# Attention scores on quadrants of TensorE's array in a fused attention and MLP kernel

## The chip, the cores and the metric

The kernel runs on one core of one Trainium2 chip. The metric is device time in microseconds of one execution; the time of the kernel before is the median of three runs, 1028.31 us (1028.2 to 1028.95). Engines are named as the profile names them: PE is TensorE's matmul, PEld its weight load, DVE VectorE, ACT ScalarE, POOL GpSimd, SP SyncE, which issues nearly all transfers.

## The reference

Sliding-window attention with a linear bias, and an MLP behind it, all in fp32:

```
batch, heads, seq, head_dim = 8, 8, 576, 64;  window = 128
scores = q @ k.T / 8 + bias        # bias = -slope[head] * (query - key)
scores = -1e9 where not (0 <= query - key < window)
attn   = softmax(scores);  y = attn @ v
x = y as 4608 tokens of 512        # 8 heads of 64 side by side
h = x @ w_in                       # 512 -> 2048
g = h * erf(softplus(h))
out = g @ w_out                    # 2048 -> 512
```

A block of 64 queries needs the keys of its own block of 64 and of the two before it, 192 keys.

## The kernel before, in words

**Units.** The 4608 tokens are 12 chunks of 384. Of every two batches, the first 384 tokens of each make a chunk, and the two remainders of 192 make a third. A chunk has four units, one for each pair of heads; unit u is chunk u // 4 and pair u % 4, 48 in all. A unit has three blocks t of 128 queries, which are two halves of 64. The first block of an ordinary chunk has 128 keys to look at, every other one 192.

**A unit's work** (class `Attention`, method `unit`): the scores of both heads in TensorE (tile `s`, line 459); VectorE adds the bias and takes the row's extreme (L466); ScalarE makes the exponential and its sum (L476); VectorE inverts the sums (L489, L490); GpSimd scales (L499); TensorE transposes (tile `t`, L517), VectorE or ScalarE copies that out (tile `pT`); TensorE multiplies with v (tile `px`, L550); the result is split in a high and a low part as a chunk's x (L560).

**The scores before.** For head j, one product has 128 rows and 128 columns of weights: rows 0 to 63 hold the 64 dimensions of q for the first half of the queries and zeros for the second, rows 64 to 127 the other way round. The moving operand is k twice, the second copy shifted by 64 keys, so that both halves meet their own 192 keys in one product. Two products (two heads) make a block; both write one bank, columns 0 and 256. The host lays out q with its zeros and k twice for each head, 1536 columns a unit (1920 in a third chunk), loaded as one tile `qk`.

**The MLP.** Products with the first six columns of blocks of w_in run beside the attention (tile `h`, L757, and `o`, L820: the first pass); the other ten run in a second pass with fewer, recombined products (L959, L1030). Each fp32 weight is split in high and low parts, mostly on VectorE, for the first pass at the start (L592 to L615). x is also saved to DRAM (tile `xd`) for the second pass.

**What sets the order.** Class `Plan` simulates the engines with a cost for each operation and a due time `at`, and writes the program out in the order that this gives. Each engine then runs its instructions in that order and waits on semaphores. `unit_time(u)` gives a unit's due time; loads are due `LL` = 22 us ahead. The line with `op({"PE": ...}, products, ...)` gives the planner the cost of a block's products; the named buffers of a tag (`Buf`) are taken in the order of use, or, with `keep=0`, by whoever comes first when one is free.

**Banks of PSUM.** Eight: two under tag "h", three under "o0" to "o2", and one each under "s" (scores), "t" (transposes) and "xt" (the product with v). In the first six units (`early`) scores also use "h", and transposes "o1". In the second pass all six of "o0" to "o2", "xt", "s" and "t" collect the output.

**Warm-up.** 40 products on zeros (L394) have the lowest priority; the planner puts them where TensorE would be idle in the first microseconds.

Of the kernel before, what the change touches and what calls it, by code (L numbers as in the profile page):

```python
# [8 lines left out]
F32 = mybir.dt.float32  # L9
# [8 lines left out]
B, H, S, D = 8, 8, 576, 64  # L18
NPAIR = H // 2
P = 128  # L20
WIN = 128
DM = H * D
# [3 lines left out]
CH = 384  # L26
NTT = CH // P
# [14 lines left out]
TE, NE = 5.5, 8  # L42
TA = 6.5
LL, LN, LT = 22, 0.3, 0
LEAD = 45
TMF = 1.2
TM = TMF * 4 * TA / NF1
# [279 lines left out]
def fp32_us(n):  # L327
    return 2 * max(n / 1200.0 + 0.003, 0.111)
# [10 lines left out]
def dma(nbytes, n=1, run=1536, eng="SP", out=False):  # L339
    packet = 9 + 0.0367 * run  # L340
    return dict(costs={eng: n * 0.42}, moved=nbytes / run * packet / 16e3 + 0.05 * n * (run > 2048), packet=packet, after=0.9 if out else 1.8 if run > 2048 else 1.3, count=n)
# [17 lines left out]
class Attention:  # L359
# [43 lines left out]
    def load(self, u):  # L403


        c, g = u // 4, u % 4
        nc, op = self.nc, self.plan.op
        at = unit_time(u) - LL
        last = c % 3 == 2
        n, m = (576, 10) if last else (384, 6)  # L410
        i = c // 3 if last else c - c // 3
        src, vsrc = self.qk[last][i, g], self.v[last][i, g]
        qk = Buf(self.kp, [P, 768 + 2 * 576], F32, "qk", NKB, f"qk{u}")
        v = Buf(self.vp, [P, 10, 2, D], F32, "v", NQ, f"v{u}")
        q = lambda t, j: qk[:, (2 * t + j) * P : (2 * t + j + 1) * P]
        k = lambda j, x, w: qk[:, 768 + j * n + x : 768 + j * n + x + w]
        if u:
            parts = [[qk]] * 3
            op(emit=lambda e: nc.sync.dma_start(qk[:, : 768 + 2 * n], src), w=[qk], at=at,
               **dma(P * (768 + 2 * n) * 4, run=(768 + 2 * n) * 4))  # L420
        else:
            both = lambda x, lo, hi: x[:, 768 : 768 + 2 * n].rearrange("p (j n) -> p j n", j=2)[:, :, lo:hi]
            pieces = [Part(qk, i) for i in range(4)]
            for i, (eng, issue, lo, hi) in enumerate((
                    ("SP", nc.sync, 0, 2 * P), ("Act", nc.scalar, 0, P), ("Act", nc.scalar, P, n), ("SP", nc.sync, 2 * P, 6 * P))):
                get = (lambda x, lo=lo, hi=hi: x[:, lo:hi]) if eng == "SP" else (lambda x, lo=lo, hi=hi: both(x, lo, hi))
                run = (hi - lo) * 4
                op(emit=lambda e, issue=issue, get=get: issue.dma_start(get(qk), get(src)), w=[pieces[i]], at=-30 + i,
                   **dma(P * run * (1 if eng == "SP" else 2), run=run, eng=eng))
            parts = [pieces[:2], pieces, pieces]  # L430
        op(emit=lambda e: nc.sync.dma_start(v[:, :m].rearrange("p x j d -> p (x j d)"), vsrc), w=[v], at=at + 2,
           **dma(P * m * 2 * D * 4, run=m * 2 * D * 4))
        return parts, q, k, v

    def unit(self, u):
# [12 lines left out]
        for t in range(3):  # L448
            c0 = 0 if last or t else 1
            n = (3 - c0) * D  # L450
            off = 192 * t if last else max(0, 128 * t - 64)
            pool, tag, bufs = (self.moe.ps_h, "h", 2) if early and (3 * u + t) % 3 else (self.ps, "s", 1)
            ps = Buf(pool, [P, 2, 256], F32, tag, bufs, f"s{u}_{t}")
            pt = Buf(self.pp, [P, 3, 2, D], F32, "p", PB, f"p{u}_{t}")
            p.append(pt)

            def products(e, ps=ps, t=t, off=off, n=n):
                for j in range(2):
                    nc.tensor.matmul(ps[:, j, :n], lhsT=q(t, j), rhs=k(j, off, n),  # L459
                                     start=True, stop=True)  # L460

            op({"PE": 2 * fp32_us(n) + 0.005}, products, r=loaded[t], w=[ps], at=at)

            def biased(e, ps=ps, pt=pt, t=t, c0=c0, n=n):
                for j in range(2):
                    nc.vector.tensor_tensor_reduce(  # L466
                        out=pt[:, c0:, j, :], in0=ps[:, j, :n].rearrange("p (c d) -> p c d", d=D),
                        in1=self.bias[g][:, j, 0::3] if c0 else self.bias[g][:, j, 1:],
                        scale=-0.125, scalar=3.0e38, op0=ALU.add, op1=ALU.min,
                        accum_out=low[t][:, j : j + 1],  # L470
                    )

            def exps(e, pt=pt, t=t, c0=c0):
                for j in range(2):
                    dst = pt[:, c0:, j, :]
                    nc.scalar.activation(dst, dst, AF.Exp, bias=low[t][:, j : j + 1], scale=-1.0,  # L476
                                         accum_out=sums[t][:, j : j + 1])

            op({"DVE": 2 * (0.07 + n * 0.0011)}, biased, r=[ps, self.bias[g]], w=[pt, low[t]], at=at)
            op({"Act": 2 * (0.285 + n * 0.00082)}, exps, tail=0.1, r=[pt, low[t]], w=[pt, sums[t]], at=at)  # L480

        at += LN
# [25 lines left out]
        parts = []  # L508
        for t in range(3):
            c0 = 0 if last or t else 1  # L510
            tag = "o1" if early and t % 2 else "t"
            ps = Buf(self.moe.ps_o if tag == "o1" else self.ps, [P, 512], F32, tag, 1, f"t{u}_{t}")

            def transposes(e, t=t, c0=c0, ps=ps):
                two = ps[:, : 2 * 192].rearrange("p (l c) -> p l c", c=192)
                for cb in range(c0, 3):
                    nc.tensor.matmul(  # L517
                        two[:, :, (2 - cb) * D : (3 - cb) * D],
                        lhsT=p[t][:, cb].rearrange("p j d -> p (j d)"), rhs=self.ident[:, :],
                        is_transpose=True, start=True, stop=True)  # L520

            op({"PE": 0.109 * (3 - c0) + 0.005}, transposes, r=[p[t]], w=[ps], at=at)
            w = (3 - c0) * D
            step, x = (192, t * 384) if not last else ((192, 0), (192, 576), (576, 384))[t]
            part = Part(pT, slice(None), t)
            parts.append(part)

            def out(e, ps=ps, w=w, step=step, x=x):
                two = ps[:, : 2 * 192].rearrange("p (l c) -> p l c", c=192)
                self.copy(e, run(x, 2, step)[:, :, :w], two[:, :, :w])  # L530

            op({"DVE": dve(2 * w), "Act": act(2 * w, src=0.053)}, out, r=[ps], w=[part], at=at)

        px = Buf(self.ps, [P, 512], F32, "xt", 1, f"px{u}")
        if last:
            todo = [[(3 * s, kk, 5 * s + kk) for s in range(2) for kk in (2, 0, 1, 3, 4)]]
        else:
# [154 lines left out]
class Moe:  # L692
# [223 lines left out]
    def second_pass(self, weights, pool2, gone, time):  # L916
# [6 lines left out]
        tiles = []  # L923
        for c in range(nc2):
            x = xs
            po = [Buf(pool, [P, DM], F32, tag, 1, f"p{tag}_{c}") for pool, tag in (
                *((self.ps_o, f"o{t}") for t in range(NTT)), *((self.ps_a, t) for t in ("xt", "s", "t")))]
            for j in range(npair):
                at = time(c * npair + j)
                if j == 1 and c + 1 < nc2:  # L930
# [196 lines left out]
def _layout(q, k, v, moe_w_in, moe_w_out):  # L1127
# [2 lines left out]
    nb = q.shape[0]  # L1130
    nch = nb * S // CH
    qT, kT = (np.ascontiguousarray(a.transpose(0, 1, 3, 2)).reshape(nb, NPAIR, 2, D, S) for a in (q, k))
    qs = np.zeros((nch, NPAIR, 2, D, 3, 2, 2, D), np.float32)
    k_a = np.zeros((nb, NPAIR, 2, D, 2, 2 * WIN + P), np.float32)
    k_c = np.zeros((nb // 2, NPAIR, 2, D, 2, 3, 192), np.float32)
    vs = np.zeros((nb, NPAIR, 2, D, S // D, 2, D), np.float32)
    heads = lambda a: a.transpose(0, 2, 1, 3)
    for b in range(nb):
        m, s = b // 2, b % 2
        for half in range(2):  # L1140
            for t in range(4):
                x = 64 * (2 * t + half)
                to = (3 * m + s, t) if t < 3 else (3 * m + 2, s)
                qs[to[0], :, half, :, to[1], :, half] = heads(qT[b, ..., x : x + 64])
            k_a[b, :, half, :, :, 64 * (1 - half) :] = heads(kT[b, ..., : 320 + 64 * half])
            x = 256 + 64 * half
            k_c[m, :, half, :, :, s] = heads(kT[b, ..., x : x + 192])
        qs[3 * m + 2, :, s, :, 2, :, s] = heads(qT[b, ..., 512:])
        k_c[m, :, s, :, :, 2] = heads(kT[b, ..., 384:])
        for j in range(2):  # L1150
            vs[b, :, j, :, :, j] = v[b, j::2].reshape(NPAIR, S // D, D, D).transpose(0, 2, 1, 3)
    qs = qs.reshape(nb // 2, 3, NPAIR, P, 768)
    qk_a = np.concatenate([qs[:, :2].reshape(nb, NPAIR, P, 768), k_a.reshape(nb, NPAIR, P, 768)], 3)
    qk_c = np.concatenate([qs[:, 2], k_c.reshape(nb // 2, NPAIR, P, 1152)], 3)
    v_a = np.ascontiguousarray(vs[..., :6, :, :]).reshape(nb, NPAIR, P, 768)
    v_c = np.concatenate([vs[s::2, ..., 4:, :, :].reshape(nb // 2, NPAIR, P, 640) for s in range(2)], 3)
    bits = lambda a: a.view(np.int64)
# [29 lines left out]
```

## Time and profile before

| | |
|---|---|
| median of three runs | 1028.31 us |
| profiled execution, its own time | 1027.85 us |
| its span | 1026.1 us |
| TensorE busy (PE) | 1010.0 us, 98% |
| weight loads (PEld) | 925.9 us, 90% |
| VectorE | 646.0 us, 63% |
| ScalarE | 647.3 us, 63% |
| GpSimd | 162.9 us, 16% |
| last score on TensorE | 464.5 us |
| moved by DMA | 191 MB, mean 186 GB/s |
| granted TensorE clock | 1.00 throughout |

The profiled execution's time is 1.75 us over its span, which runs from the first instruction to the last. Rows of the timeline give the start in us, the length in us, engine, line and operation, tile written and tiles read, the shape of the product (rows times columns of weights), the moving operand, and how many instructions were merged. A product in fp32 shows as two weight loads and two matmul rows; one in the rounded form (fp32r, the MLP's) as one of each. The length of a matmul row is modelled and reaches into its successor's; distances between starts say how fast rows follow each other.

### The profile page before, as it was taken

The numbers are of one execution on the slowest core, as the hardware profiler recorded it, in microseconds if no ns is written. First come the engines' busy times: TensorE is split into PE (matmuls) and PEld (weight loads), VectorE is DVE, ScalarE is ACT, GpSimd is POOL, SyncE is SP. The second block draws the span as 40 slices with busy tenths as digits, with TensorE's granted clock in tenths as the row PEclk, the third lists the DMA queues.
The fourth block names the chain that finished last, engine by engine and source line by source line (L and its number), as shares of the span: only waits on it lengthen the run. The fifth ranks groups of instructions, "written<-read, shape, count | busy, mean of one in ns | idle before, by whom it ended". The sixth has DMA issues, their size and how long they took to land.

```text
span 1026.1 us, 16045 instructions
## 1 busy us (share of the span) xinstructions
PE 1010.0 (98%) x5612; PEld 925.9 (90%) x5612; DVE 646.0 (63%) x1554; ACT 647.3 (63%) x1302; POOL 162.9 (16%) x294
## 2 busy tenths in 40 slices
PE   9899999999999999999999999999999999999998
PEld 8889999888999899999999989889989899899896
DVE  4999888778888645546356547447456456454433
ACT  5788668666787657565557664664665655555543
POOL 3454442225342232211000000000000000000000
PEclk9999999999999999999999999999999999999999
DMA  9865879788969554545778333323323324320402
GB/s 369 331 211 196 306 238 320 243 305 289 345 238 346 174 195 159 181 159 190 291 279 307 124 110 116 113 97 130 113 84 143 113 72 148 121 64 29 124 1 72
DMA packets 63761, 190.98 MB, mean 186 GB/s; under 512 B 7105, under 2 KB 7873, under 8 KB 63681
## 3 DMA queue, kind: packets, MB, share of 16 engines
q1 hardware_dynamic: 62992, 189.43, 52.6%
q8 instruction: 45, 0.74, 0.3%
q10 hardware_dynamic: 688, 0.52, 0.2%
q14 instruction: 36, 0.29, 0.1%
HBM read 137.76 MB, written 52.17 MB: 185 GB/s over the span
## 4 chain that ended last, share of the span: by engine, by line
PE 81%; DVE 12%; DMA 3%; issue 2%; ACT 1%; POOL 0%; DVEq 0%; POOLq 0%; SPq 0%; ACTq 0%
PE pa L959 12%; PE po L1030 12%; PE o L820 11%; PE h L757 10%; PE pc L959 6%; PE px L550 5%; PE s L459 5%; PE pxt L1030 4%; PE pt L1030 4%; PE ps L1030 4%; PE pb L959 3%; DVE p L466 3%; PE t L517 2%; PE warm_ps L394 1%; DMA wd<-wto 1%
## 5 line engine op out<-in xcount | busy, mean ns | idle before, releaser
L499 POOL TENSOR_SCALAR p<-p,st 128x192 f32<-128x192 f32 (+1 forms) x288 | 162.2, 581 | 306.4 <-DVE st L490 204.9
L757 PE MATMUL h<-x,wi 128*128 128x384 f32 x864 | 175.7, 345 | 0.3 <-DVE st L466 0.3
L740 ACT COPY hs<-pa 128x384 f32<-128x384 f32 x115 | 55.2, 480 | 175.0 <-PE pa L959 175.0
L757 PEld LDWEIGHTS h<-x,wi 128*128 128x128 f32 x864 | 150.5, 188 | 3.4 <-PE s L459 0.5
L476 ACT ACTIVATE p<-p,st 128x192 f32<-128x192 f32 (+1 forms) x288 | 124.9, 436 | 41.7 <-DVE st L466 41.3
L820 PE MATMUL o<-wo,gh 128*128 128x512 f32 x432 | 145.5, 418 | 0.0
L459 PE MATMUL s<-qk 128*128 128x192 f32 (+1 forms) x576 | 110.5, 316 | 2.5 <-DVE st L466 2.0
L959 PE MATMUL pa<-t,p 128*128 128x384 f32 x540 | 108.4, 335 | 0.0
L550 PEld LDWEIGHTS px<-pT,v 128*128 128x128 f32 x704 | 100.7, 191 | 3.2 <-DVE pT L401 1.2
L550 PE MATMUL px<-pT,v 128*128 128x192 f32 (+2 forms) x704 | 102.6, 295 | 0.6 <-DVE pT L401 0.4
L1010 DVE TENSOR_TENSOR hs<-s,hs 128x768 f32<-128x768 f32 x60 | 54.8, 953 | 72.3 <-ACT s L1002 72.3
L959 PEld LDWEIGHTS pa<-t,p 128*128 128x128 f32 x540 | 95.5, 187 | 3.4 <-ACT hs L740 0.3
L459 PEld LDWEIGHTS s<-qk 128*128 128x128 f32 x576 | 90.9, 190 | 7.5 <-issue 2.7
L1030 PE MATMUL po<-ho,gh 128*128 128x512 f32 x270 | 90.8, 390 | 0.0
L970 DVE TENSOR_TENSOR hs<-pc,hs 128x384 f32<-128x384 f32 x60 | 33.4, 557 | 90.0 <-PE pc L959 48.7
L466 DVE CUSTOM_DVE_ANT_0 p<-s,bias 128x192 f32<-128x192 f32 x224 | 70.4, 351 | 29.0 <-PE s L459 22.7
L820 PE MATMUL o<-wo,gl 128*128 128x512 f32 x216 | 85.3, 395 | 0.0
L820 PEld LDWEIGHTS o<-wo,gh 128*128 128x128 f32 x432 | 75.4, 189 | 7.1
L517 PE MATMUL t<-ident,p 128*128 128x128 f32 x400 | 67.2, 274 | 7.5 <-POOL p L499 4.0
L1030 PE MATMUL po<-ho,gl 128*128 128x512 f32 x180 | 71.4, 397 | 0.0
L399 ACT COPY pT<-t 128x384 f32<-128x384 f32 (+1 forms) x87 | 39.5, 455 | 48.0 <-PE t L517 40.4
L517 PEld LDWEIGHTS t<-ident,p 128*128 128x128 f32 x400 | 50.2, 144 | 18.5 <-POOL p L499 8.0
(272 smaller groups left out, 1825.5 us busy)
## 6 DMA issues: line engine op xcount, KB each, us to landing
qk<-qk_a SPq DMA_DIRECT2D x31, 768.0 KB, 6.7
xd<-x SPq DMA_DIRECT2D x24, 768.0 KB, 6.0
qk<-qk_c SPq DMA_DIRECT2D x16, 960.0 KB, 5.9
v<-v_a SPq DMA_DIRECT2D x32, 384.0 KB, 4.4
v<-v_c SPq DMA_DIRECT2D x16, 640.0 KB, 4.3
pd<-ot SPq DMA_DIRECT2D x36, 256.0 KB, 3.8
out<-pd SPq DMA_DIRECT2D x36, 256.0 KB, 3.4
p<-wd SPq DMA_DIRECT2D x35, 256.0 KB, 5.0
```

The costliest lines, as they stand in the source:

```text
L459: nc.tensor.matmul(ps[:, j, :n], lhsT=q(t, j), rhs=k(j, off, n), start=True, stop=True)
L466: nc.vector.tensor_tensor_reduce(out=pt[:, c0:, j, :], in0=ps[:, j, :n].rearrange("p (c d) -> p c d", d=D), in1=self.bias[g][:, j, 0::3] i ...
L476: nc.scalar.activation(dst, dst, AF.Exp, bias=low[t][:, j : j + 1], scale=-1.0, accum_out=sums[t][:, j : j + 1])
L499: nc.gpsimd.tensor_scalar(dst, dst, sums[t][:, j : j + 1], 1.0, op0=ALU.mult, op1=ALU.mult)
L517: nc.tensor.matmul(two[:, :, (2 - cb) * D : (3 - cb) * D], lhsT=p[t][:, cb].rearrange("p j d -> p (j d)"), rhs=self.ident[:, :], is_transp ...
L550: nc.tensor.matmul(px[:, to : to + m * D], lhsT=v[:, blk].rearrange("p j d -> p (j d)"), rhs=run(src, m, 256)[:, :, :D], start=first and x ...
L740: self.nc.scalar.copy(out, src)
L757: nc.tensor.matmul(ps[:, :CH], lhsT=ww[:, cs], rhs=xx[:, k], start=(k2 + k + n == 0), stop=(k2 + k + n == 4),)
L820: nc.tensor.matmul(po.all, lhsT=g[:, j, cs], rhs=w.all, start=(u["start"] and n == 0), stop=(u["end"] and n == 2),)
L959: nc.tensor.matmul(dst[:, :CH], lhsT=wv[i](k), rhs=xb[l][:, k], start=start and k + n == 0, stop=k + n == 3, skip_group_check=not start)
L1010: op({"DVE": dve(2 * CH)}, lambda e, s=s, hs=hs: V.tensor_tensor(hs.all, s.all, hs.all, ALU.mult), r=[s, *parts], w=parts, at=at, port=True)
L1030: nc.tensor.matmul(po.all, lhsT=g[:, k, cs], rhs=w.all, start=start and n == 0, stop=end and n == 2)
```

## The change

For each block, four products take the place of two, one for each pair of head j and half h. Head j's q and k lie in rows 64 j to 64 j + 63 of the tile `qk`, once and without zeros. The weights are 64 dimensions by 64 queries, the moving operand 64 dimensions by 192 (or 128) keys, and the product lies on the quadrant of the array that its rows (head) and its output's partitions (half) give. The four are written in the order (j, h) = (0, 0), (1, 0), (0, 1), (1, 1). Each head has its own bank, so a block takes two. The planner's cost for a block is now `SQ` (0.2) plus that of one product in place of two.

A unit's load has 832 columns (384 of q, 448 of k, the first 64 of k zeros) in place of 1536, and in a third chunk 1024 in place of 1920. The first unit's load is still cut in four pieces, the first two of which the first block needs.

The three banks "s", "t" and "xt" become one tag "a" of three, taken by whichever operation comes and finds enough free: two for scores, one for a transpose, one for the product with v. In the first six units scores go in turn to "a", to the two of "h", and to "o0" and "o2". VectorE's biasing reads one bank for each head. The shapes of all other operations stay.

```diff
+SQ = 0.2
...
-        n, m = (576, 10) if last else (384, 6)
+        n, m = (640, 10) if last else (448, 6)
...
-        qk = Buf(self.kp, [P, 768 + 2 * 576], F32, "qk", NKB, f"qk{u}")
+        qk = Buf(self.kp, [P, CH + 640], F32, "qk", NKB, f"qk{u}")
...
-        q = lambda t, j: qk[:, (2 * t + j) * P : (2 * t + j + 1) * P]
-        k = lambda j, x, w: qk[:, 768 + j * n + x : 768 + j * n + x + w]
+        rows = lambda j: slice(j * D, (j + 1) * D)
+        q = lambda t, j, h: qk[rows(j), t * P + h * D : t * P + (h + 1) * D]
+        k = lambda j, x, w: qk[rows(j), CH + x : CH + x + w]
...
-            op(emit=lambda e: nc.sync.dma_start(qk[:, : 768 + 2 * n], src), w=[qk], at=at,
-               **dma(P * (768 + 2 * n) * 4, run=(768 + 2 * n) * 4))
+            op(emit=lambda e: nc.sync.dma_start(qk[:, : CH + n], src), w=[qk], at=at, **dma(P * (CH + n) * 4, run=(CH + n) * 4))
...
-            off = 192 * t if last else max(0, 128 * t - 64)
-            pool, tag, bufs = (self.moe.ps_h, "h", 2) if early and (3 * u + t) % 3 else (self.ps, "s", 1)
-            ps = Buf(pool, [P, 2, 256], F32, tag, bufs, f"s{u}_{t}")
+            if last:
+                off = [320 * t, 320 * t + D] if t < 2 else [P, 320 + P]
+            else:
+                off = [max(0, t * P - D) + x for x in (0, D)]
+            place = (0, 1, 2)[(3 * u + t) % 3] if early else 0
+            if place == 0:
+                ps = [Buf(self.ps, [P, 512], F32, "a", 3, f"s{u}_{t}{j}", keep=0) for j in range(2)]
+            elif place == 1:
+                ps = [Buf(self.moe.ps_h, [P, 512], F32, "h", 2, f"s{u}_{t}{j}") for j in range(2)]
+            else:
+                ps = [Buf(self.moe.ps_o, [P, 512], F32, f"o{2 * j}", 1, f"s{u}_{t}{j}") for j in range(2)]
...
-                for j in range(2):
-                    nc.tensor.matmul(ps[:, j, :n], lhsT=q(t, j), rhs=k(j, off, n),
-                                     start=True, stop=True)
-
-            op({"PE": 2 * fp32_us(n) + 0.005}, products, r=loaded[t], w=[ps], at=at)
+                for h in range(2):
+                    for j in range(2):
+                        nc.tensor.matmul(ps[j][h * D : (h + 1) * D, :n], lhsT=q(t, j, h), rhs=k(j, off[h], n),
+                                         start=True, stop=True)
+
+            op({"PE": SQ + fp32_us(n)}, products, r=loaded[t], w=ps, at=at)
...
-                        out=pt[:, c0:, j, :], in0=ps[:, j, :n].rearrange("p (c d) -> p c d", d=D),
+                        out=pt[:, c0:, j, :], in0=ps[j][:, :n].rearrange("p (c d) -> p c d", d=D),
...
-            tag = "o1" if early and t % 2 else "t"
-            ps = Buf(self.moe.ps_o if tag == "o1" else self.ps, [P, 512], F32, tag, 1, f"t{u}_{t}")
+            spare = early and t % 2
+            ps = Buf(self.moe.ps_o, [P, 512], F32, "o1", 1, f"t{u}_{t}") if spare else Buf(
+                self.ps, [P, 512], F32, "a", 3, f"t{u}_{t}", keep=0)
...
-        px = Buf(self.ps, [P, 512], F32, "xt", 1, f"px{u}")
+        px = Buf(self.ps, [P, 512], F32, "a", 3, f"px{u}", keep=0)
...
+    gap = np.zeros((nb, NPAIR, 2, D, D), np.float32)
+    qk_a = flat(np.concatenate([qT[..., :CH], gap, kT[..., :CH]], 4))
```

More of the change, by code (lines that the diff above doesn't have):

```diff
@@ L409, in load @@
         last = c % 3 == 2
-        n, m = (576, 10) if last else (384, 6)
+        n, m = (640, 10) if last else (448, 6)
         i = c // 3 if last else c - c // 3
         src, vsrc = self.qk[last][i, g], self.v[last][i, g]
-        qk = Buf(self.kp, [P, 768 + 2 * 576], F32, "qk", NKB, f"qk{u}")
+        qk = Buf(self.kp, [P, CH + 640], F32, "qk", NKB, f"qk{u}")
         v = Buf(self.vp, [P, 10, 2, D], F32, "v", NQ, f"v{u}")
-        q = lambda t, j: qk[:, (2 * t + j) * P : (2 * t + j + 1) * P]
-        k = lambda j, x, w: qk[:, 768 + j * n + x : 768 + j * n + x + w]
+        rows = lambda j: slice(j * D, (j + 1) * D)
+        q = lambda t, j, h: qk[rows(j), t * P + h * D : t * P + (h + 1) * D]
+        k = lambda j, x, w: qk[rows(j), CH + x : CH + x + w]
         if u:
             parts = [[qk]] * 3
-            op(emit=lambda e: nc.sync.dma_start(qk[:, : 768 + 2 * n], src), w=[qk], at=at,
-               **dma(P * (768 + 2 * n) * 4, run=(768 + 2 * n) * 4))
+            op(emit=lambda e: nc.sync.dma_start(qk[:, : CH + n], src), w=[qk], at=at, **dma(P * (CH + n) * 4, run=(CH + n) * 4))
         else:
-            both = lambda x, lo, hi: x[:, 768 : 768 + 2 * n].rearrange("p (j n) -> p j n", j=2)[:, :, lo:hi]
             pieces = [Part(qk, i) for i in range(4)]
             for i, (eng, issue, lo, hi) in enumerate((
[L425 to L429, printed above, removed]
+                    ("SP", nc.sync, 0, P), ("Act", nc.scalar, CH, CH + 192), ("Act", nc.scalar, CH + 192, CH + n), ("SP", nc.sync, P, CH))):
+                op(emit=lambda e, issue=issue, lo=lo, hi=hi: issue.dma_start(qk[:, lo:hi], src[:, lo:hi]), w=[pieces[i]], at=-30 + i,
+                   **dma(P * (hi - lo) * 4, run=(hi - lo) * 4, eng=eng))
             parts = [pieces[:2], pieces, pieces]
@@ L477, in exps @@
                                          accum_out=sums[t][:, j : j + 1])
-            op({"DVE": 2 * (0.07 + n * 0.0011)}, biased, r=[ps, self.bias[g]], w=[pt, low[t]], at=at)
+            op({"DVE": 2 * (0.07 + n * 0.0011)}, biased, r=[*ps, self.bias[g]], w=[pt, low[t]], at=at)
             op({"Act": 2 * (0.285 + n * 0.00082)}, exps, tail=0.1, r=[pt, low[t]], w=[pt, sums[t]], at=at)
@@ L925, in second_pass @@
             x = xs
-            po = [Buf(pool, [P, DM], F32, tag, 1, f"p{tag}_{c}") for pool, tag in (
-                *((self.ps_o, f"o{t}") for t in range(NTT)), *((self.ps_a, t) for t in ("xt", "s", "t")))]
+            po = [Buf(self.ps_o, [P, DM], F32, f"o{t}", 1, f"po{t}_{c}") for t in range(NTT)]
+            po += [Buf(self.ps_a, [P, DM], F32, "a", 3, f"pa{t}_{c}", keep=0) for t in range(NTT)]
             for j in range(npair):
@@ L1132, in _layout @@
     qT, kT = (np.ascontiguousarray(a.transpose(0, 1, 3, 2)).reshape(nb, NPAIR, 2, D, S) for a in (q, k))
-    qs = np.zeros((nch, NPAIR, 2, D, 3, 2, 2, D), np.float32)
-    k_a = np.zeros((nb, NPAIR, 2, D, 2, 2 * WIN + P), np.float32)
-    k_c = np.zeros((nb // 2, NPAIR, 2, D, 2, 3, 192), np.float32)
+    flat = lambda a: a.reshape(a.shape[0], NPAIR, P, a.shape[-1])
+    gap = np.zeros((nb, NPAIR, 2, D, D), np.float32)
+    qk_a = flat(np.concatenate([qT[..., :CH], gap, kT[..., :CH]], 4))
+    both = lambda a, lo, hi: [a[s::2, ..., lo:hi] for s in range(2)]
+    qk_c = flat(np.concatenate([*both(qT, CH, 512), *both(qT, 512, S), *both(kT, 256, S)], 4))
     vs = np.zeros((nb, NPAIR, 2, D, S // D, 2, D), np.float32)
-    heads = lambda a: a.transpose(0, 2, 1, 3)
     for b in range(nb):
[L1139 to L1149, printed above, removed]
         for j in range(2):
             vs[b, :, j, :, :, j] = v[b, j::2].reshape(NPAIR, S // D, D, D).transpose(0, 2, 1, 3)
-    qs = qs.reshape(nb // 2, 3, NPAIR, P, 768)
-    qk_a = np.concatenate([qs[:, :2].reshape(nb, NPAIR, P, 768), k_a.reshape(nb, NPAIR, P, 768)], 3)
-    qk_c = np.concatenate([qs[:, 2], k_c.reshape(nb // 2, NPAIR, P, 1152)], 3)
     v_a = np.ascontiguousarray(vs[..., :6, :, :]).reshape(nb, NPAIR, P, 768)
```

## The prediction

> **What bounds the kernel now.** I read the windows by stage first, then the page's chain, then the timeline of TensorE around single score blocks, and last the waits.
>
> ```profile
> core 0: us, PE busy (x) PEld busy (x) DVE busy (x) ACT busy (x) POOL busy (x), PEclk, DMA share, GB/s
> 0.00:25.00 25.00, 23.04 (x161) 22.35 (x162) 11.88 (x65) 14.93 (x52) 8.16 (x24) 1.00 0.94 368
> 25.00:100.00 75.00, 70.03 (x440) 65.16 (x439) 74.41 (x237) 59.26 (x165) 32.05 (x45) 1.00 0.66 241
> 100.00:475.00 375.00, 369.94 (x2258) 344.69 (x2257) 270.97 (x863) 260.68 (x681) 122.66 (x226) 1.00 0.72 252
> 475.00:1026.10 551.10, 547.00 (x2760) 493.70 (x2758) 288.79 (x392) 312.48 (x405) 0.00 (x0) 1.00 0.37 125
> ```
>
> Each row is a stretch; after the times come busy us and instructions per engine. Up to 25 us TensorE is filled up with warm-up products and the DMA engines are 0.94 busy. From 25 to 100 us VectorE has 74.41 of 75 us: it sets the pace, TensorE has 5 us free. From 100 us on TensorE is 98.7% busy, so there a microsecond of its work is a microsecond of the end. Behind 475 us no score is left. The scores alone, in the same stretches:
>
> ```profile
> 0.00:25.00 25.00, 6.07 (x36) 5.33 (x36) 1.00 0.94 368
> 25.00:100.00 75.00, 21.27 (x111) 17.24 (x112) 1.00 0.66 241
> 100.00:475.00 375.00, 83.20 (x431) 68.30 (x429) 1.00 0.72 252
> ```
>
> A score block is four rows of TensorE (two products, each run twice in fp32: 576 rows for 288 products), so 9 blocks lie in the first stretch, 28 in the second, 107 of the 144 in the third. The busy times overlap with neighbours; what a block costs is read from starts:
>
> ```profile
> 251.20 0.81 PE L459 MATMUL s<-qk 128*128 128x192 f32 x4
> 251.85 0.38 PE L517 MATMUL t<-ident,p 128*128 128x128 f32 x2
> ...
> 255.43 0.52 PEld L459 LDWEIGHTS s<-qk 128*128 128x128 f32 x4
> 255.88 0.30 PEld L820 LDWEIGHTS o<-wo,gh 128*128 128x128 f32 x2
> ...
> L459 PE MATMUL s<-qk 128*128 128x192 f32 x448 | 91.3, 328 | 2.0 <-DVE st L466 2.0
> L459 PE MATMUL s<-qk 128*128 128x128 f32 x128 | 19.7, 276 | 0.6 <-PE s L459 0.6
> ```
>
> A block of 192 columns holds the array 251.85 - 251.20 = 0.65 us, 0.163 a row; one of 128 columns 255.88 - 255.43 = 0.45 us, 0.11 a row. A row lasts 328 ns though the next starts 163 ns later: some 0.16 us of a row is a tail that its successor hides. 448 rows are 112 blocks, 128 rows are 32.
>
> **The change part by part.** *The products.* Two products of 128 dimensions by 128 queries, half of them zeros, become four of 64 by 64 on the array's quadrants, in the order of rows 0-63, 64-127, 0-63, 64-127. This is the piece of TensorE's order before, at the 25th unit:
>
> ```order
> L459 MATMUL s_0_2706<-qk_2438 128x128 x2
> L820 MATMUL o_12_2290<-wo_1298,gh_2570 128x512 x2
> L820 MATMUL o_12_2290<-wo_1298,gl_2579 128x512
> L757 MATMUL h_2719<-x_0_1665,wi_887 128x384 x6
> L459 MATMUL s_1_2738<-qk_2438 128x192 x2
> ```
>
> and the same unit now (s_10 and s_11 are block 1 of heads 0 and 1, each written twice, in its upper and lower half):
>
> ```order
> L466 MATMUL s_00_3178<-qk_2831 64x128
> L466 MATMUL s_01_3180<-qk_2831 64x128
> L466 MATMUL s_00_3178<-qk_2831 64x128
> L466 MATMUL s_01_3180<-qk_2831 64x128
> L765 MATMUL h_3141<-x_1_2660,wi_857 128x384 x6
> L466 MATMUL s_10_3202<-qk_2831 64x192
> L466 MATMUL s_11_3204<-qk_2831 64x192
> L466 MATMUL s_10_3202<-qk_2831 64x192
> L466 MATMUL s_11_3204<-qk_2831 64x192
> ```
>
> A block stays between full-array work on both sides; only what stands in it moves. The trace has no product on a quadrant, so its cost is bounded. Below: all four at once, as long as one product: two rows, 0.33 us at 192 columns, 0.22 at 128. Above: one after another, eight rows: 1.30 us, and 8 x 0.109 = 0.87. Between them the question is when the last quadrant starts. Six weight loads stand ahead of its first one's. A load of 128 columns sets the pace of the short block, 0.11 us; one of 64 I take at half, 0.055. If quadrants in different rows load side by side, the last starts 3 x 0.055 = 0.165 us late; if all load in turn, 0.33. I take 0.165, since a product can be taken up while its forerunner still streams, as here:
>
> ```profile
> 255.54 0.61 PE L459 MATMUL s<-qk 128*128 128x128 f32 x4
> 255.90 0.48 PE L820 MATMUL o<-wo,gh 128*128 128x512 f32 x1
> ```
>
> Four rows from 255.54, 0.11 apart, put the last score at 255.87; the next product's row opens 0.03 us behind it, 0.08 before the score has streamed, and is long (0.48) for the wait within it. So TensorE does look past a product that is not done. Block: 0.165 + 0.33 = 0.49 us at 192 columns, 0.385 at 128. Saved: 0.163 x 112 + 0.065 x 32 = 18.3 + 2.1 = 20.4 us of TensorE.
>
> *Where it counts.* In the first stretch nothing, for warm-up products fill in; in the second nothing, for VectorE's biasing is the same work:
>
> ```profile
> L466 DVE CUSTOM_DVE_ANT_0 p<-s,bias 128x192 f32<-128x192 f32 x224 | 70.4, 351 | 29.0 <-PE s L459 22.7 <-POOL p L499 4.3 <-PE t L517 1.2
> ...
> 150.00:200.00 50.00, 48.67 (x299) 45.41 (x298) 37.91 (x120) 37.41 (x93) 15.58 (x30) 1.00 0.86 305
> 200.00:250.00 50.00, 47.27 (x293) 43.76 (x292) 41.44 (x126) 31.26 (x91) 16.42 (x25) 1.00 0.85 294
> ```
>
> So 107/144 of 20.4 = 15.1 us. From 150 to 250 us TensorE already lacks work for 4.1 us, and of the some 4 us that its 29 blocks would save there I let half go to longer waits: 15.1 - 2 = 13.
>
> *q without zeros, k once.* A load shrinks from 1536 columns to 832, one for a third chunk from 1920 to 1024, SyncE's queue before and now:
>
> ```order
> L419 DMA qk_243<-qk_a 128x1536
> L431 DMA v_246<-v_a 128x768
> L419 DMA qk_251<-qk_a 128x1536
> L584 DMA wri_258<-w_in 128x1024
> L584 DMA wri_262<-w_in 128x1024
> ```
>
> ```order
> L421 DMA qk_243<-qk_a 128x832
> L429 DMA v_246<-v_a 128x768
> L421 DMA qk_251<-qk_a 128x832
> L592 DMA wri_254<-w_in 128x1024
> L592 DMA wri_258<-w_in 128x1024
> ```
>
> ```profile
> qk<-qk_a SPq DMA_DIRECT2D x31, 768.0 KB, 6.7
> qk<-qk_c SPq DMA_DIRECT2D x16, 960.0 KB, 5.9
> ...
> 7.70 0.61 PE L459 MATMUL s<-qk 128*128 128x128 f32 x4
> ```
>
> The order is kept, the loads are shorter: by 832/1536 and 1024/1920, 768 KB becomes 416 and 960 becomes 512, so 32 x 352 + 16 x 448 KB = 18.4 MB less (the first load is cut in four pieces and not in the 31). Only ahead of 25 us are the DMA engines full, and there VectorE waits for the first scores, which start at 7.70 us. Bounds 0 and 1 us; I take 0.5, since it carries over into VectorE's own stretch. Later transfers hide under TensorE's work either way.
>
> *Three banks shared.* A block takes two of them where scores, transposes and output had one each. Biasing must have read both (2 x 0.35 us) before another block opens. What it can cost is bounded by the waits now: TensorE waited for VectorE ahead of scores 2.0 us in all (the row of L459 above), and other work stands between blocks; below nothing, above 0.35 us for each of 107 blocks, 37 us, were each queued behind one read. I take 0.5 us, nearest to the row.
>
> Sum: -13 - 0.5 + 0.5 = -13 us on the profiled execution's 1027.85 (span 1026.1 and 1.75 around it), which is 0.46 below the median of 1028.31: 1015 us.
>
> **The rivals.** *In order, two at a time.* Each product is two rows on the same quadrant, and the second cannot stream beside the first. If TensorE starts rows strictly in order, the next quadrant waits behind that second row, and only a second row and the next first row ever run together: five spacings, 0.815 us at 192 columns, 5 x 0.109 = 0.545 at 128. That is 0.163 x 112 + 0.095 x 32 = 21.3 us more, 107/144 of it 15.8, and some 1 us of the stretch before, where TensorE has 5 us free for its 4 us more: about 1045 us. For it speaks that all rows above start in order; against it the product taken up early. The Trainium skill, "TensorE: Matmul & The Clock Gate", section "The mechanism", has matmuls strictly first in, first out, in start and end; by that rule this rival holds. The trace agrees as far as the order of starts goes; no run here has quadrants.
>
> *The array is emptied on each change of its division.* Then a block pays a row's tail on the way in and out, 2 x 0.165 us. The 144 blocks stand in 133 runs between full-array work, counted in the new order: 44 us against 20.4 saved, 23 net, of which 107/144 = 17 and a part of the rest: about 1047 us. Against it: scores, transposes and the other products follow each other without a gap now, though none changes the division. The Trainium skill, "TensorEngine Tiling (Array Packing)", section "Key Properties", states that a change of tiling mode drains TensorE; by it this rival holds. No run here shows it.
>
> *It does not do what it says.* If all loads go in turn, the block lasts 0.33 + 0.33 = 0.66 us at 192 columns, as before, and 0.55 at 128, 0.1 x 32 x 107/144 = 2.4 us more: 1028 to 1031.
>
> *No two at once:* 0.65 x 112 + 0.42 x 32 = 86 us more, nearly 107/144 of it 64, and what TensorE's 5 free us do not take of the rest: about 1100 us.
>
> **How the numbers follow.** My forecast, 1015 us: 0.50. In order by twos, 1045: 0.24. Emptied, 1047: 0.12. No gain, 1028 to 1031: 0.10. No overlap, 1100: 0.04. The forecast's own range is 1003 (start offsets half as long and the DMA gain whole) to 1024 (a third of the saving). For 8 in 10 I take 1003 to 1051, both slower rivals' centres included. Under 0.2%, 2 us, this kernel's measurement tells no change. Faster by more: 0.50 and a fifth of the fourth case, 0.52; same 0.06; slower 0.42.
>
> **What would show it.** In the changed trace the starts of a block's eight rows: the last quadrant's first row about 0.165 us behind the block's first says I am right, 0.49 us (three spacings) or more says in order. The distance from a block's last row to the next full product, against 0.163 within it, shows emptying. Waits of TensorE ahead of scores for VectorE, above 2 us in all, show the banks. VectorE in 25 to 100 us should stay full. I am wrong if a block of 192 columns holds the array for 0.6 us or more.

## The result, and the profile after

The changed kernel takes 1042.34 us (1039.5 to 1043.94) where the kernel before takes 1028.26: ratio 1.014, 95% interval 1.0112 to 1.0168. It is 14 us slower; the forecast was 13 us faster. The profiled execution has a span of 1040.2 us. Two of the runs below each have one execution at a lower granted clock (the loads alone, 1881.71 us at 0.82; the first one of one run a unit, 1081.23 us at 0.86), which their medians include and their ratios leave out.

The windows by stage of the changed kernel, columns as in those of before:

```profile
core 0: us, PE busy (x) PEld busy (x) DVE busy (x) ACT busy (x) POOL busy (x), PEclk, DMA share, GB/s
0.00:25.00 25.00, 21.82 (x182) 17.94 (x182) 10.95 (x63) 14.43 (x52) 8.20 (x22) 1.00 0.93 357
25.00:100.00 75.00, 66.60 (x502) 53.88 (x503) 70.77 (x220) 53.65 (x147) 28.77 (x44) 0.98 0.45 151
100.00:475.00 375.00, 373.70 (x2680) 301.74 (x2679) 272.91 (x856) 262.23 (x683) 131.87 (x214) 1.00 0.62 215
475.00:510.00 35.00, 34.37 (x229) 29.86 (x227) 16.92 (x38) 19.28 (x43) 11.57 (x17) 1.00 0.33 126
510.00:600.00 90.00, 85.82 (x430) 77.93 (x430) 44.59 (x60) 55.96 (x71) 0.00 (x0) 0.96 0.74 272
```

Three things are new. TensorE is even fuller from 100 to 475 us (373.70 against 369.94), though its work was to shrink. GpSimd still works behind 475 us: the attention's scaling now reaches into that stretch. And the granted clock (PEclk), 1.00 everywhere before, is 0.98 and 0.96 in two stretches; in 510 to 600 us TensorE is also idle for 4.2 us. Before, that last stretch read so:

```profile
510.00:600.00 90.00, 90.00 (x456) 81.70 (x455) 46.85 (x65) 59.98 (x75) 0.00 (x0) 1.00 0.61 215
```

**A block on the quadrants.** TensorE's timeline around one block of the changed kernel: first, from a narrow piece of the timeline, the first four rows of the block; then, from another piece, the second four; then the weight loads of what follows:

```profile
251.17 0.62 PE L828 MATMUL o<-wo,gh 128*128 128x512 f32 x2
251.63 0.40 PE L828 MATMUL o<-wo,gl 128*128 128x512 f32 x1
251.96 0.39 PE L466 MATMUL s<-qk 64*64 64x192 f32 x4
...
252.17 0.34 PE L466 MATMUL s<-qk 64*64 64x192 f32 x4
...
252.44 0.30 PEld L828 LDWEIGHTS o<-wo,gh 128*128 128x128 f32 x2 [0.28 <-issue]
252.78 0.19 PEld L828 LDWEIGHTS o<-wo,gl 128*128 128x128 f32 x1
```

Four rows start within the merged 251.96: their starts are 7 ns apart, one on each quadrant. The second row of every product comes 0.21 us later, again all four together. So the four quadrants do run at once, and the rows are not taken in the order in which they are written: the first rows of all four products go ahead of the second row of the first. A row does not name its product, but two rows of a block raise a semaphore. In the program these are the second rows of the third and of the fourth product, the sixth and the eighth row written; in the trace they are the seventh and the eighth to start.

But look at both ends. The product ahead starts at 251.63 and streams for 0.23 us (the two rows before it start at 251.17 and 251.40), so until 251.86; the block's first row starts at 251.96, and its stream, I take it, only when its weights are in. The last of the block's second rows starts 0.02 us behind the first and streams until some 252.35, and the next weights are asked for at 252.44 and not during the stream: PEld shows a gap of 0.28 us, where before the change loads ran under the products ahead. The second of the two products that follow begins to stream at 252.78, as the load behind it starts; the first, of 0.23 us, so begins at 252.55. So the block holds the array from 251.86 to 252.55, 0.69 us. Worked out like this for every block that stands alone (medians; the blocks before by the same rule):

| | before | after |
|---|---|---|
| 192 columns | 0.656 us (101 blocks) | 0.689 us (103) |
| 128 columns | 0.453 us (28) | 0.582 us (27) |

That is 0.033 x 112 + 0.129 x 32 = 7.8 us more of TensorE in place of 20.4 us less: 0.33 (or 0.22) us of streaming and 0.36 us at the ends. It is so if each of the 144 blocks stands alone; as they stand in 133 runs, 11 pairs of ends fall away, and some 4 us are left.

**What comes late.** TensorE's waits in the changed kernel (for whom, us in all, times, longest):

```profile
PE t L525 <- POOL p L506: 9.1, 13, 1.4
PE pa L967 <- issue: 4.2, 1, 4.2
PE s L466 <- DVE st L473: 1.1, 2, 0.9
```

and the same kind of row before:

```profile
PE t L517 <- POOL p L499: 4.0, 5, 1.5
```

The second row is one wait, ahead of the second pass's first product. The view by tile gives the first and last start of the attention's last operation, px, before and after, and SyncE's timeline the first fetch of the second pass's weights (p<-wd) behind the last save of x:

```profile
L550 PE MATMUL px<-pT,v x704: 218/299/431, 19.3 to 494.0; 128*128 128x192 f32 x80, 128*128 128x128 f32 x64, 128*128 128x64 f32 x32
...
495.48 0.32 SPq L732 DMA_DIRECT2D xd<-x  x1
495.96 3.86 SPq L680 DMA_DIRECT2D p<-wd  x7
```

```profile
L558 PE MATMUL px<-pT,v x704: 218/300/431, 18.0 to 514.0; 128*128 128x192 f32 x80, 128*128 128x128 f32 x64, 128*128 128x64 f32 x32
...
515.40 0.32 SPq L740 DMA_DIRECT2D xd<-x  x1
515.91 0.32 SPq L688 DMA_DIRECT2D p<-wd  x1
```

The attention ends 20 us later, and so the fetches start 20 us later, since the second pass's weights take over the attention's memory. Behind most of these weights stands the fetch of the first block of x that the second pass reads (`11_0`, from `xd`):

```profile
551.02 0.32 SPq L905 DMA_DIRECT2D 11_0_6521<-xd  x1
...
DMA to landing us min/median/max: 6.6/6.6/6.6
...
557.73 0.98 PE L967 MATMUL pa<-11_0_6521,p 128*128 128x384 f32 x2 [4.18 <-issue]
```

It lands at 557.6 us, and that ends the wait. Before, the same block landed at 531.0 us for a product at 544.2. The first pass's last products stand behind that wait in TensorE's order; they end 13 us later than before (last o at 569.2 and 582.1 us).

In sum, the span is 14.1 us longer. TensorE is idle for 5.7 us more (21.8 against 16.1): 4.2 at this wait, 4.7 ahead of 100 us and 0.6 from 475 to 510, less 3.8 from 100 to 475. It is busy for 8.4 us more (1018.4 against 1010.0): by estimate 4 for the ends of the blocks and 4.4 for two stretches at half the clock, worked out at the end.

### The profile page after: what moved, and what is told of

It reads as the page before. It is cut to its first block, busy times and chain, and to the rows that moved or that the text cites. A ratio compares the mean times of both kernels' runs of the same rounds, so it can differ in the third digit from the quotient of the medians.

```text
span 1040.2 us, 17155 instructions
## 1 busy us (share of the span) xinstructions
PE 1018.4 (98%) x6188; PEld 873.7 (84%) x6188; DVE 644.7 (62%) x1547; ACT 649.3 (62%) x1309; POOL 180.4 (17%) x294
## 4 chain that ended last, share of the span: by engine, by line
PE 90%; POOL 4%; DVE 2%; ACT 2%; issue 1%; POOLq 0%; DVEq 0%
PE o L828 14%; PE h L765 13%; PE pa L967 12%; PE po L1038 12%; PE pa L1038 12%; PE px L558 8%; PE pc L967 6%; PE s L466 5%; POOL p L506 4%; PE t L525 3%; PE pb L967 3%; PE warm_ps L395 1%; DVE p L473 1%; ACT p L483 1%; ACT s L796 0%
## 5 line engine op out<-in xcount | busy, mean ns | idle before, releaser
L506 POOL TENSOR_SCALAR p<-p,st 128x192 f32<-128x192 f32 (+1 forms) x288 | 179.7, 642 | 326.7 <-DVE st L497 185.2
L828 PEld LDWEIGHTS o<-wo,gh 128*128 128x128 f32 x432 | 73.1, 191 | 22.4 <-issue 15.0
L1038 PE MATMUL pa<-ho,gh 128*128 128x512 f32 x270 | 90.6, 389 | 0.0
L466 PE MATMUL s<-qk 64*64 64x192 f32 (+1 forms) x1152 | 77.3, 335 | 1.5 <-DVE st L473 1.1
L525 PE MATMUL t<-ident,p 128*128 128x128 f32 x400 | 63.6, 277 | 9.1 <-POOL p L506 9.1
L1038 PE MATMUL pa<-ho,gl 128*128 128x512 f32 x180 | 70.2, 390 | 0.0
```

Source lines behind the costliest of these rows:

```text
L466: nc.tensor.matmul(ps[j][h * D : (h + 1) * D, :n], lhsT=q(t, j, h), rhs=k(j, off[h], n), start=True, stop=True)
L506: nc.gpsimd.tensor_scalar(dst, dst, sums[t][:, j : j + 1], 1.0, op0=ALU.mult, op1=ALU.mult)
L525: nc.tensor.matmul(two[:, :, (2 - cb) * D : (3 - cb) * D], lhsT=p[t][:, cb].rearrange("p j d -> p (j d)"), rhs=self.ident[:, :], is_transp ...
L828: nc.tensor.matmul(po.all, lhsT=g[:, j, cs], rhs=w.all, start=(u["start"] and n == 0), stop=(u["end"] and n == 2),)
L1038: nc.tensor.matmul(po.all, lhsT=g[:, k, cs], rhs=w.all, start=start and n == 0, stop=end and n == 2)
```

## The experiments

Several theories were still open when the trace had ruled out rows in strict order. **A**: a run of quadrant products has some 0.36 us at its two ends, whatever it holds, and the rest of the loss comes from the order that the shared banks bring. Against it, **B**: all of the loss is in the products; **C**: all of it is in the banks and the order; **F**: the surplus goes with each product or load and not with the ends of a run. All ratios are to the kernel before on the same chip.

### Full products in the changed kernel's order

```diff
-                for h in range(2):
-                    for j in range(2):
-                        nc.tensor.matmul(ps[j][h * D : (h + 1) * D, :n], lhsT=q(t, j, h), rhs=k(j, off[h], n), ...)
+                for j in range(2):
+                    nc.tensor.matmul(ps[j][:, :n], lhsT=full(t * P, P), rhs=full(CH + off[0], n), ...)
```

The planner keeps the changed kernel's costs, so every engine's order stays.

> The changed kernel, in its own order, with its banks, loads and waits, but each block computed by two products on the whole array (128 rows by 128 columns, both heads' rows summed) in place of four on quadrants; so the heads are not kept apart and the scores are not the reference's. Theory A (a run of quadrant products costs some 0.36 us at its two ends beside 0.33 or 0.22 us of streaming, so that a block holds the array 0.69 us where a full one holds 0.656, and 0.583 where 0.453; the rest of the loss comes from the shared banks' order): 0.034 x 112 + 0.13 x 32 = 8 us less than the changed kernel's 1042.3 at most, 6 if a quarter of it is hidden: 1034 to 1036. Rival B (all of the loss is in the products): 1028. Rival C (all of it is in the order and the banks): 1042.

Measured: 1036.42 us, ratio 1.008 (1.0065 to 1.0095), 0.4 us above what A gave. Both B and C fall: of the 1.4%, some 0.6 goes with the products (6 us, where 4 to 7.8 were reckoned; the 6 include some 1.6 us that the changed kernel's profiled execution loses at a lowered clock at 75 us and this one does not) and 0.8 with what is left, order, banks and loads. Single blocks hold the array 0.656 and 0.454 us again, so the ends are not the waits or the banks, which are the same here. What is left shows most in the last stretch, which is that of the changed kernel, wait and lowered clock included:

```profile
510.00:600.00 90.00, 85.65 (x422) 77.85 (x421) 46.29 (x63) 56.81 (x72) 0.00 (x0) 0.96 0.74 272
551.10:558.00 6.90, 6.14 (x18) 5.70 (x19) 2.69 (x4) 1.21 (x2) 0.00 (x0) 0.51 1.02 401
```

4.35 us idle and some 3 us lost in 6.14 busy us at half the clock make 7.4 us of the 8.4 by which the profiled span is longer than before. Elsewhere TensorE is idle 3.5 us more up to 100 us and 1.9 us less from there to 475.

### The banks alone

```diff
 # the kernel before, and:
-            ps = Buf(pool, [P, 2, 256], F32, tag, bufs, f"s{u}_{t}")
+            ps = [Buf(self.ps, [P, 512], F32, "a", 3, f"s{u}_{t}{j}", keep=0) for j in range(2)]  # early units as in the change
...
-        px = Buf(self.ps, [P, 512], F32, "xt", 1, f"px{u}")
+        px = Buf(self.ps, [P, 512], F32, "a", 3, f"px{u}", keep=0)   # and the transposes' bank alike
```

> The kernel before with its own products, loads and costs, and only the three banks shared, two for a block of scores. Theory A: its order, like the changed kernel's, ends the attention with less of the first pass left behind the last product with v (some 50 us in place of 60), so the weights of the second pass arrive late and TensorE waits some 4 us ahead of the second pass and runs some us at a lowered clock: 1033 to 1037. Rival B (banks cost nothing): 1028. Rival C (all of the loss is the banks): 1042.

Measured: 1037.6 us, ratio 1.0098 (1.0075 to 1.0121). The banks alone cost 10 us, 0.6 us above what A gave. Attention ends late here too, with full products and the kernel's own costs:

```profile
L556 PE MATMUL px<-pT,v x704: 218/299/430, 18.9 to 509.5; 128*128 128x192 f32 x80, 128*128 128x128 f32 x64, 128*128 128x64 f32 x32
...
510.00:600.00 90.00, 88.21 (x444) 79.32 (x443) 47.85 (x66) 55.88 (x71) 0.00 (x0) 1.00 0.75 272
100.00:475.00 375.00, 367.46 (x2221) 341.91 (x2220) 263.12 (x822) 263.16 (x675) 126.94 (x209) 1.00 0.71 248
```

The mechanism is not the one expected: the wait ahead of the second pass is missing, the idle time behind the attention is 1.8 us and the clock stays at 1.00; another 2.5 us is missing from 100 to 475 us (367.46 against 369.94). Of the 8.2 us that the profiled span is longer, the windows place 5.5 as idle time of TensorE; the rest I have not placed.

### The loads alone

```diff
 # the kernel before with the changed kernel's loads, and:
+                    nc.tensor.matmul(ps[:, j, :n], lhsT=full(t * P, P), rhs=full(CH + off[0], n), ...)
```

> The kernel before, with its banks, order and two products on the whole array per block, and only the loads of the changed kernel (832 and 1024 columns a unit), so the heads are not kept apart and the scores are not the reference's. Theory A: only the first 25 us can gain, 0 to 2 us: 1026 to 1028. Rival D (the lighter loads are worth several us that the rest of the change ate): 1024 or less. Rival E (the loads' new place makes others late): over 1029.

Measured: 1027.57 us, ratio 0.9998 (0.9986 to 1.001). 18 MB less to load is worth nothing that can be measured. D and E fall.

### One run a unit

```diff
+        starts = [(0,), (1,), (2,)] if early else [(0, 1), (2,)] if last else [(0, 1, 2)]
...
+                    for x, off, col, w_ in jobs:        # the blocks of a run, side by side in the pair of banks
+                        for h in range(2):
+                            for j in range(2):
+                                nc.tensor.matmul(ps[j][h * D : (h + 1) * D, col : col + w_], lhsT=q(x, j, h),
+                                                 rhs=k(j, off[h], w_), start=True, stop=True)
...
+                op({"PE": SR + sum(fp32_us(x[3]) for x in jobs)}, products, r=loaded[run_[-1]], w=ps, at=at)   # SR = 0.36
```

128 + 192 + 192 columns fill a bank of 512 exactly.

> The changed kernel with the quadrant products of all three blocks of a unit written one behind the other from the seventh unit on, in one pair of banks side by side (in a third chunk, blocks 0 and 1, then 2), so that the array changes its division some 66 times in place of 133. Theory A: 67 times 0.36 us less of TensorE, 24 us, of which three quarters or more count: 1018 to 1024, or some us more if the pair of banks is held too long. Rival F (the surplus goes with each product or load and not with the ends of a run): 1040 to 1043.

Measured: 1012.19 us, ratio 0.9835 (0.9812 to 0.9859). F falls, and A gave too little: the time is 6 us below its range. The same kernel once more, for its profile:

> The kernel of the one run a unit, unchanged, for a profile and a closer time. Theory A: a unit's run of three blocks holds the array some 0.36 + 0.22 + 2 x 0.33 = 1.24 us where three runs held 0.583 + 2 x 0.69 = 1.96; the time is again 14 to 17 us below the kernel before. Rival: the earlier gain was chance, and it comes out at 1020 or more.

Measured: 1008.95 us, ratio 0.9823 (0.9797 to 0.9849), 18 us below the kernel before where A had 14 to 17. It beats both kernels. A unit's run in its timeline, to compare with the block above, where eight rows start at 251.96 and the next product at 252.44:

```profile
252.68 0.86 PE L776 MATMUL h<-x,wi 128*128 128x384 f32 x4
253.47 1.10 PE L474 MATMUL s<-qk 64*64 64x128 f32 x24
254.50 0.62 PE L776 MATMUL h<-x,wi 128*128 128x384 f32 x2
```

24 rows, three blocks, take 1.03 us from their first start to the next product's, where one block takes 0.48. By the same rule as above such a run holds the array 1.234 us (median of 27), a run of two blocks of 192 columns 1.017: 0.36 + 0.22 + 2 x 0.33, and 0.36 + 2 x 0.33. Runs save 67 x 0.36 = 24 us against the changed kernel; the ratio says 32 us. The rest fits the end of the attention, which is no longer late, and the last stretch, which has the clock back; no run takes the two apart:

```profile
L569 PE MATMUL px<-pT,v x704: 218/323/687, 17.1 to 485.2; 128*128 128x192 f32 x80, 128*128 128x128 f32 x64, 128*128 128x64 f32 x32
...
510.00:600.00 90.00, 88.56 (x442) 79.43 (x442) 46.66 (x66) 54.23 (x68) 0.00 (x0) 1.00 0.62 228
```

### The products twice

```diff
-                for h in range(2):
+                for h in (0, 1, 0, 1):
```

> The changed kernel with the four quadrant products of each block written twice, the second four over the first. Theory A (0.36 us at the ends of a run, 0.33 or 0.22 us for four products at once): the second four cost 0.33 x 112 + 0.22 x 32 = 44 us more, less the part that VectorE's stretch hides: 1078 to 1086, and a block of 192 columns holds the array for 1.02 us. Rival F (0.69 and 0.58 us go with the products themselves): 96 us more, 1125 to 1138, and 1.38 us.

Measured: 1077.64 us, ratio 1.0482 (1.0459 to 1.0506), 35 us over the changed kernel and 0.4 us under A's range. F falls. From its timeline, 16 rows of a block:

```profile
252.22 0.88 PE L466 MATMUL s<-qk 64*64 64x192 f32 x16
253.03 0.44 PE L765 MATMUL h<-x,wi 128*128 128x384 f32 x1
```

The next product starts 0.81 us behind the first row, 0.33 more than with eight. Held, by medians: 1.014 us at 192 columns, 0.800 at 128, so the second four cost 0.325 and 0.218 and what is left of a block, 0.364, belongs to the ends: 0.689 - 0.325 and 0.582 - 0.218 give the same number.

### The planner told the truth

```diff
-            op({"PE": SQ + fp32_us(n)}, products, r=loaded[t], w=ps, at=at)
+            op({"PE": SQ + 0.16 + fp32_us(n)}, products, r=loaded[t], w=ps, at=at)
```

> The changed kernel with the planner told what a block really holds (0.36 us in place of 0.2 beside one product), nothing else. Theory A (the order is set by the banks, and the planner's error of 0.16 us a block matters little): 1039 to 1043. Rival G (the planner's wrong cost is what spoils the order): 1034 or less.

Measured: 1047.49 us, ratio 1.0188 (1.0171 to 1.0206): some 5 us slower than the changed kernel with the wrong cost. Neither expectation held. The attention ends at 518.0 us here, 4 us later still, and from 200 to 400 us TensorE is idle for 4.8 us (0.5 in the changed kernel) and twice at half the clock, for 3.4 us each time. So the order moves the time by several us with small changes of its inputs, and not always the way that truer inputs suggest; why the planner's order came out worse is open.

### Two blocks a run

```diff
-        starts = [(0,), (1,), (2,)] if early else [(0, 1), (2,)] if last else [(0, 1, 2)]
+        starts = [(0,), (1,), (2,)] if early else [(0, 1), (2,)]
```

> As the one run a unit, but blocks 0 and 1 in one run and block 2 in another, in ordinary chunks too: some 92 changes to quadrants in place of 133 (changed kernel) and 66 (one run a unit). Theory A: 41 x 0.36 = 15 us of TensorE less than in the changed kernel, so between the two: 1024 to 1030. Rival (one run a unit gains by something else than the number of runs): as the changed kernel, 1040, or as the one run a unit, 1012.

Measured: 1021.34 us, ratio 0.9941 (0.9922 to 0.9961), between the two as A had it, and 3 us under its range. Against the number of runs:

| runs on quadrants | ratio |
|---|---|
| 133 (the change) | 1.014 |
| 92 (two blocks) | 0.9941 |
| 66 (a unit) | 0.9823 |

Each 0.020 and 0.012 lower, so 0.50 and 0.47 us a run: the 0.36 us of the ends, and something on top that comes with the earlier end of the attention (514.0, 494.3 and 485.2 us).

### Shared banks, but one for a block

```diff
 # the kernel before, and:
+            pool, tag, bufs = (self.moe.ps_h, "h", 2) if early and (3 * u + t) % 3 else (self.ps, "a", 3)
+            ps = Buf(pool, [P, 512], F32, tag, bufs, f"s{u}_{t}", keep=1 if tag == "a" else None)
...
+        px = Buf(self.ps, [P, 512], F32, "a", 3, f"px{u}", keep=1)
```

> The kernel before with its own products and loads, the three banks shared by scores, transposes and the product with v, but a block of scores still in one bank; scores and the product with v leave one bank free for transposes. Theory A1 (what costs is that a block needs two of the three banks at once): 1028 to 1030. Theory A2 (what costs is the sharing itself, whoever comes first taking a bank, which ends the attention later in the planner's order, some 48 us of the first pass left behind it in place of 60): 1033 to 1038.

Measured: 1032.68 us, ratio 1.0047 (1.0032 to 1.0062), 0.3 us under A2's range and clear of A1. The attention ends at 506.0 us, and the wait ahead of the second pass is there, 3.7 us, with the clock at 0.96 behind it. Sharing alone costs 5 of the banks' 10 us; that a block needs two banks at once would be the other 5, though the rule by which one bank is left free differs too, so the split is not clean.

## Why the prediction was wrong

*The step that failed* is the block's cost, "0.165 + 0.33 = 0.49 us at 192 columns, 0.385 at 128". Its second term was right (0.325 measured, 0.218 at 128). The first, the late start of the last quadrant, measured 0.02 us: four starts 7 ns apart, so the six weight loads ahead of it do not stand in its way. (Nor did the rows before show that loads set the short block's pace: 128 columns at the pace of the long block, 192 in 0.163 us, also take 0.109.) What was missing from the sum is the ends, 0.36 us a run: the block holds the array for 0.689 and 0.582 us in place of 0.49 and 0.385. I had them as a rival, with the trace's hidden tail as their price, 2 x 0.165 = 0.33, and gave it 0.12, because no row of the trace before showed a gap between kinds of products. But no two of those kinds divide the array differently, so those rows said nothing about it. The size of that rival was right; the weight was the mistake. The Trainium skill, "TensorEngine Tiling (Array Packing)", section "Key Properties", says that a change of tiling mode drains TensorE and that tiles operate independently; the trace agrees with both, with 0.36 us a run and starts 7 ns apart.

*In order, two at a time*, had 1045 us, near the time measured, and is ruled out all the same: the last quadrant's first row would have started 0.49 us behind the first, and started 0.02 us behind it. The right time for a wrong reason, by luck: the starts tell, not the total. The Trainium skill, "TensorE: Matmul & The Clock Gate", section "The mechanism", has matmuls start strictly in the order written; here the trace differs. In the written order the second row of the first product stands ahead of the first row of the second product, and it started some 0.2 us behind it.

*The emptied array at 1047* had the mechanism, with other terms: 20.4 us saved and 44 lost. Measured, the streaming saves 44.6 us and the ends cost 48 to 52, a net of 4 to 8 us of TensorE and 6 of time; the other 8 came from elsewhere. That its time is so near was in part luck.

*The shared banks* were the other failed term: "I take 0.5 us, nearest to the row", where the banks alone cost 10 us. The bound above, 37 us, held. I looked for the price at the wait that I could name, scores behind VectorE; that wait fell to 1.1 us. What the runs show is another order from the planner: the attention ends 12 to 20 us later in the changed kernel, with full products in its order, with the banks alone and with one bank for a block. The order's rows around the 25th unit, that I quoted, cannot show that. How the 10 us come about stays open in part: three of the four have the wait ahead of the second pass, but the banks alone do not, and only 5.5 of the 8.2 us there are placed.

*The loads*: half a us taken, nothing measurable found; right. *Nothing up to 100 us, VectorE full from 25*: wrong. VectorE is busy 70.77 of 75 us, so no longer full, TensorE is idle for 4.7 us more up to 100 us, and it waits more for GpSimd's scaling (9.1 us in all against 4.0). The loads alone do not show this (TensorE is idle there for 5.4 us up to 100 us, and 6.9 before); full products in the changed kernel's order do (10.5).

*The low end, 1003 us*: with the 2 us that the sum lets go to waits it comes out at 1005; nothing hangs on it.

*The signs* given for the emptying (0.25 us from the block's last row to the next product, against 0.163 within the blocks before) and for the block of 0.6 us or more (0.689) were the right ones. That for the banks, waits for VectorE, was not.

## What to carry to other kernels

Between products on the whole array, quadrants paid here only in runs: at 0.36 us for the two ends and 0.33 us for four products that took 0.65 as two, one block a run loses, two already win. Put as many of them as the banks' columns hold side by side into one run. And where banks are pooled in a kernel whose order a planner makes, look at when each stage ends, and not only at waits for banks: sharing three banks cost some 8 to 10 us here, more than the 6 us of the products that had been changed.

## What the runs showed of the hardware that was not expected

TensorE took eight rows, written as first and second row of four products in turn, in another order: four first rows 7 ns apart, then four second rows. And the granted clock fell right behind short idle times. Of the changed kernel:

```profile
71.80:75.20 3.40, 1.68 (x8) 0.97 (x8) 3.40 (x10) 2.28 (x7) 3.40 (x5) 1.00 0.00 0
75.20:78.60 3.40, 3.26 (x9) 2.68 (x10) 2.69 (x6) 0.00 (x0) 0.09 (x1) 0.50 0.00 0
553.10:556.50 3.40, 0.45 (x3) 0.03 (x1) 1.47 (x2) 3.37 (x4) 0.00 (x0) 0.99 1.04 404
556.50:563.30 6.80, 5.57 (x16) 5.14 (x17) 2.74 (x4) 1.84 (x3) 0.00 (x0) 0.50 1.03 403
```

A stretch of 3.4 us in which TensorE was busy half of the time, or hardly at all, is followed by 3.4 or 6.8 us at half the clock. At that clock 3.26 busy us lose 1.6, and 5.57 lose 2.8. So 1.7 us of waiting cost another 1.6 us, and the 4.2 us ahead of the second pass another 2.8. The same shows in other runs, with 1.54 to 1.94 us busy in the 3.4 us ahead (the loads alone, one run a unit, the planner told the truth, two blocks a run). How much idle time it takes was not measured.
